# Two batches' last 64 tokens in one product with w_theta, and a new order of work around it

## The chip, the core and the metric

The program runs on one core of a Trainium2 chip. That core has five engines with an instruction stream each: TensorE (PE; matmuls and the loads of their stationary side), VectorE (DVE), ScalarE (ACT), GpSimd (POOL) and SyncE (SP), which here only issues transfers. TensorE writes its results to PSUM banks, and DVE and ACT read them from there. The metric is the device time of one execution in microseconds.

## The reference

There are 8 batches of 576 tokens. Attention comes first: 8 heads of 64 channels, keys and values averaged over groups of 8 tokens, so that 576 queries meet 72 pooled keys. The result, 576 tokens by 512 channels per batch, is the input x of a mixing block.

```python
def _attn_ref(q, k, v):                       # (8, 8, 576, 64) each
    k_p = k.reshape(B, H, 72, 8, D).mean(axis=3)
    v_p = v.reshape(B, H, 72, 8, D).mean(axis=3)
    scores = scale * np.matmul(q, k_p.transpose(0, 1, 3, 2))
    attn = softmax(scores)                    # written out with max, exp and sum
    return np.matmul(attn, v_p)

def _moe_ref(x, w_theta, w_tok_r, w_tok_i, w_ch):
    theta = x @ w_theta
    zr, zi = x * np.cos(theta), x * np.sin(theta)
    y = np.einsum('ts,bsd->btd', w_tok_r, zr) + np.einsum('ts,bsd->btd', w_tok_i, zi)
    u = x + y
    return u + np.maximum(u @ w_ch, 0.0)
```

All inputs are 32-bit floats. The product with w_theta takes a token's 512 channels to 512 angles. It is done for each token by itself, so tokens of different batches may share a product.

## The kernel before, in words

Every operand of a large product is split into a high and a low part, and three of the four partial products are added in PSUM. One "product" of a token block with w_theta (`pt`, line 888) is therefore 12 matmuls: 3 terms by 4 blocks of 128 channels. The stationary side is 128 tokens of x, the moving side 512 columns of w_theta.

The work of a batch b is written as Python generators ("streams"), each of which yields after each step. One long text, `SCHEDULE` (lines 30 to 131), names the stream whose next step comes next, and with a letter at the end (v, a or g) the engine that does it. So the order of each engine's instructions, the transfers of SP among them, is the order of the words in that text. Nothing is reordered later; an engine whose next instruction must wait holds up all that stand behind it. The words, for batch b:

- `k`, `v`, `Q` load keys, values and queries, `K` and `V` pool them and put them in place.
- `Sb.m` (`soften`): scores of token block m in bank pair `s`, maximum, exponential, sum, division, and a transpose into the buffer `G`. Blocks 0 to 3 have 128 tokens, block 4 has 64.
- `Eb.0`, `Eb.2` (`turn`): for blocks 0 and 1, or 2, 3 and 4, sixteen transfers on SP from `G` to the single buffer `eraw`, and the split into high and low.
- `Xb.g.c` (`attend`): four matmuls for channel block c, giving x (bank `av`; 256 tokens for g = 0, 320 for g = 2), then a copy out of the bank. After the last c of g = 2 the last 64 tokens are copied once more, so that block 4 of x has 128 columns, each token twice.
- `Tb.m` (`rotate`): for token block m the split of x, the product `pt` (bank `th`), its rounding on ACT and DVE (tile `g`), four transposes of x (bank `px`), sine and cosine on ACT, and the products with x into `z`. In block 4 the two copies of a token give sine and cosine at once, by a bias that differs between the two halves (`c_half`).
- `Zb.c` (`take`), `Mb.c.hf` (`mix`): the split of z, 27 matmuls with the token weights for 256 (hf = 0) or 320 tokens (hf = 1), in one of two banks `mm`, and u = x + y with its split.
- `Fb.c.hf` (`final`): 12 matmuls with w_ch, the sum, a transpose into `R`; after the second half four transfers to the output.

M of a batch reads z of all of its tokens, so it comes after all five T of the batch. The steady part of the order overlaps M and F of batch b with T of batch b + 1 and S, E and X of batch b + 2 or b + 1. The banks `av`, `th`, `px`, `s` and the tiles `g`, `sn`, `G`, `eraw` exist once; x exists twice (tag `xT`, one tile of 640 columns for each batch), the splits `xh` and `xl` of a block twice.

Of the kernel before, what the change touches and what calls it, by code (L numbers as in the profile page):

```python
# [9 lines left out]
F32 = mybir.dt.float32  # L10
# [71 lines left out]
T3.3 T3.3 T3.3 F2.2.0 F2.2.0 F2.2.1 F2.2.1 F2.2.1 V5.0g T3.3 T3.3a T3.3 E4.0g E4.0g V4g T3.3 T3.3 S4.3g S4.3g  # L82
S4.4 K5a T3.4 T3.4 T3.4 T3.4 T3.4 T3.4 F2.3.0 Q5.1 Q5.1 T3.4 F2.3.1 F2.3.1 F2.2.1 E4.0g F2.3.0 K5 K5a X4.0.0
S5.0 X4.0.0v F2.3.0 F2.3.1 X4.0.1 X4.0.1a Z3.0g Z3.0v M3.0.0 M3.0.0 S4.3 Z3.1a Z3.1g S4.4 S4.4 S4.4g S4.4g S5.0
X4.0.2 X4.0.2a S4.4 v5.1 M3.0.0v M3.0.0v V5.1g M3.0.1 M3.0.1 M3.0.1g M3.0.1g X4.0.3 X4.0.3a T4.0v T4.0v Z3.2a
Z3.2g M3.1.1 M3.1.1 M3.1.1a M3.1.1v T4.0 T4.0 T4.0 T4.0 S5.1 v5.2 V5.2g S5.0 S5.0 S5.0v S5.0v S5.1 S5.1 M3.1.0
M3.1.0 M3.1.0a M3.1.0v S5.1 Z3.3a Z3.3v T4.0 T4.0a M3.2.0 k6.0 M3.2.0 M3.2.0v M3.2.0g E4.2 E4.2g S5.0 M3.3.0
M3.3.0 M3.3.0v E4.2a E4.2g E4.2v M3.2.1 M3.2.1 X4.2.2 M3.3.0g X4.2.2a M3.2.1v F3.0.0 F2.3.1 S5.1v X4.2.0 X4.2.0a
F3.0.0 S5.1v S5.1 k6.2 K6.2v K6.0g T4.1v T4.1v M3.3.1 M3.3.1 M3.3.1g M3.3.1g X4.2.1 X4.2.1a F3.0.0 Q6.0 S5.2
S5.2 X4.2.3 k6.1 T4.0 T4.0 T4.0 V5a V5g X4.2.3v T4.1 V5 M3.2.1g K6.1g T4.1 E5.0 T4.1 T4.1 T4.1 T4.1a T4.1 T4.2v  # L90
# [40 lines left out]
"""

EARLY, EXACT, V_ON_PE, K_ON_PE, Q_ON_PE, SUMS_ON_ACT = 2, 1, 1, 1, 2, 2


@with_exitstack
def tile_attn_moe(  # L140
# [832 lines left out]
    def final(b, c, hf):  # L973
# [30 lines left out]
        if hf == 0:  # L1004
            return
# [123 lines left out]
```

## Time and profile before

| | |
|---|---|
| median of the runs | 630.47 us (630.33 to 631.11, 3 runs) |
| the profiled execution | 629.07 us, its span 627.3 us |
| TensorE busy | 591.2 us, 94% of the span, 4120 matmuls |
| DVE, ACT, POOL busy | 77%, 50%, 56% |
| granted TensorE clock, mean | 0.996 |

A row of the order of time gives the start, the time from first start to last end, the engine, the line, the operation, output and inputs with shapes, and the count of instructions merged in it. In brackets stands how long the engine was idle before it and what ended the wait. A row of a group gives busy time, the mean of one in ns, and the idle time before. Matmuls overlap, so that the distance from the start of one to the start of the next is shorter than the length of either.

### The profile page before, as it was taken

What the parts mean: (1) busy time and instruction counts of PE and PEld (TensorE: products, weight loads), DVE (VectorE), ACT (ScalarE), POOL (GpSimd) and SP (SyncE); (2) the same over time, 40 slices, a digit from 0 to 9 for tenths busy, and PEclk for the clock granted to TensorE, in tenths of its full rate; (3) what the DMA queues carried; (4) which work ended last, traced back from release to release, by engine and by line L of the source; (5) the groups of instructions that cost most, each with busy time, mean ns of one, the idle gap of its engine ahead of it and who ended that gap; (6) DMA issues with size and microseconds to landing.
All of it is one profiled execution on the core that took longest, in us unless ns stands there. A gap on an engine that the chain in (4) does not pass through costs nothing.

```text
span 627.3 us, 11459 instructions
## 1 busy us (share of the span) xinstructions
PE 591.2 (94%) x4120; PEld 545.7 (87%) x4120; DVE 481.5 (77%) x878; ACT 312.6 (50%) x674; POOL 350.2 (56%) x380
## 2 busy tenths in 40 slices
PE   4889979999899999899999999999999999999995
PEld 4766769988799879899899989989998999998995
DVE  5599988988897889878967898877886689456433
ACT  4769857688742556247534553237314451345000
POOL 5346545756484656565574667667675375611430
PEclk9999999999999999999999999999999999999999
DMA  9946212475465556554726356443362340511015
GB/s 295 266 135 190 67 43 77 81 124 118 91 125 99 98 100 125 100 95 82 129 58 108 63 107 120 75 85 56 52 100 51 68 65 5 79 20 30 9 20 77
DMA packets 235129, 57.85 MB, mean 92 GB/s; under 512 B 223168, under 2 KB 223680, under 8 KB 235072
## 3 DMA queue, kind: packets, MB, share of 16 engines
q1 hardware_dynamic: 233888, 56.97, 45.2%
q8 instruction: 33, 0.54, 0.4%
q10 hardware_dynamic: 1184, 0.15, 0.2%
q14 instruction: 24, 0.20, 0.1%
HBM read 37.81 MB, written 9.44 MB: 75 GB/s over the span
## 4 chain that ended last, share of the span: by engine, by line
PE 59%; DVE 14%; SPq 10%; DMA 7%; ACT 4%; issue 3%; POOL 3%; DVEq 0%; POOLq 0%; ACTq 0%
PE py L954 24%; PE pf L983 12%; PE pt L888 11%; SPq L814 8%; PE pv L861 4%; PE s L670 3%; DMA out_dram<-R 2%; PE px L898 2%; DMA eraw<-G 1%; DMA WTh_st<-in_moe_w_theta_dram 1%; SPq L1008 1%; DVE kpst L443 1%; DVE R L1002 1%; DMA kpst<-in_k_dram 1%; DVE xT L960 1%
## 5 line engine op out<-in xcount | busy, mean ns | idle before, releaser
L954 PE MATMUL py<-WTh,zh 128*128 128x256 f32 (+1 forms) x576 | 86.5, 297 | 4.4 <-DVE xT L960 2.8
L954 PE MATMUL py<-WTl,zh 128*128 128x256 f32 (+1 forms) x576 | 87.3, 296 | 0.0
L954 PE MATMUL py<-WTh,zl 128*128 128x256 f32 (+1 forms) x576 | 86.0, 294 | 1.0 <-DVE xT L960 1.0
L954 PEld LDWEIGHTS py<-WTh,zh 128*128 128x128 f32 x576 | 80.1, 189 | 5.3 <-DVE xT L960 3.0
L954 PEld LDWEIGHTS py<-WTl,zh 128*128 128x128 f32 x576 | 80.4, 190 | 0.0
L954 PEld LDWEIGHTS py<-WTh,zl 128*128 128x128 f32 x576 | 78.0, 188 | 1.6 <-DVE xT L960 1.2
L940 POOL TENSOR_TENSOR zl<-z,zh 128x640 fp32r<-128x640 f32 (+1 forms) x40 | 59.5, 1509 | 29.4 <-ACT zh L175 28.9
L967 POOL TENSOR_TENSOR ul<-xT,uh 128x320 fp32r<-128x320 f32 (+1 forms) x41 | 34.6, 849 | 43.6 <-DVE uh L177 29.1
L960 DVE TENSOR_TENSOR xT<-py,xT 128x256 f32<-128x256 f32 (+1 forms) x64 | 28.4, 445 | 35.1 <-PE py L954 35.0
L892 ACT ACTIVATE g<-pt,c_magic 128x512 f32<-128x512 f32 x38 | 26.1, 686 | 44.6 <-PE pt L888 36.2
L983 PE MATMUL pf<-uh,chh 128*128 128x256 f32 (+1 forms) x256 | 47.1, 305 | 0.3 <-DVE xT L960 0.3
L888 PE MATMUL pt<-th,xh 128*128 128x512 f32 x160 | 45.3, 405 | 1.4 <-DVE g L894 0.8
L983 PE MATMUL pf<-ul,chh 128*128 128x256 f32 (+1 forms) x256 | 44.8, 296 | 0.0
L983 PE MATMUL pf<-uh,chl 128*128 128x256 f32 (+1 forms) x256 | 44.5, 296 | 0.0
L894 DVE SCALAR_TENSOR_TENSOR g<-g,pt 128x512 f32<-128x512 f32 x38 | 25.8, 680 | 24.1 <-ACT g L892 23.8
L175 ACT CAST uh<-xT 128x320 fp32r<-128x320 f32 (+1 forms) x28 | 12.0, 434 | 63.2 <-DVE xT L960 63.1
L888 PE MATMUL pt<-th,xl 128*128 128x512 f32 x160 | 43.3, 393 | 0.0
L725 ACT ACTIVATE e_eps<-e_eps 128x576 f32<-128x576 f32 (+1 forms) x30 | 20.6, 686 | 45.4 <-DVE e_eps L721 45.3
L888 PE MATMUL pt<-tl,xh 128*128 128x512 f32 x160 | 43.1, 391 | 0.0
L865 ACT ACTIVATE xT<-pv 128x320 f32<-128x320 f32 (+1 forms) x41 | 16.8, 410 | 51.3 <-PE pv L861 45.6
L881 POOL TENSOR_TENSOR xl<-xT,xh 128x512 fp32r<-128x512 f32 x22 | 30.0, 1368 | 20.2 <-ACT xh L175 16.6
L989 DVE SCALAR_TENSOR_TENSOR oT<-pf,xT 128x256 f32<-128x256 f32 (+1 forms) x64 | 28.5, 449 | 14.2 <-PE pf L983 13.5
(252 smaller groups left out, 1491.6 us busy)
## 6 DMA issues: line engine op xcount, KB each, us to landing
out_dram<-R SPq DMA_DIRECT2D x112, 72.0 KB, 2.1
kpst<-in_k_dram SPq DMA_DIRECT2D x15, 512.0 KB, 3.9
vpst<-in_v_dram SPq DMA_DIRECT2D x28, 256.0 KB, 3.9
qsst<-in_q_dram SPq DMA_DIRECT2D x96, 72.0 KB, 2.4
eraw<-G SPq DMA_DIRECT2D x96, 60.0 KB, 2.2
eraw<-G SPq DMA_DIRECT2D x96, 40.0 KB, 2.1
WTh_st<-in_moe_w_theta_dram SPq DMA_DIRECT2D x4, 512.0 KB, 8.6
wcraw<-in_moe_w_ch_dram SPq DMA_DIRECT2D x4, 512.0 KB, 3.3
```

Source lines behind the costliest of these rows:

```text
L814: nc.sync.dma_start(blocks(Ex, jj, i), blocks(Gx, i, jj))
L861: nc.tensor.matmul(pv[:, :gn], l, r, start=i == 0, stop=i == len(terms) - 1)
L881: ENG[pick()].tensor_tensor(xl, xT[:, :, o], f32(xh), ALU.subtract)
L888: nc.tensor.matmul(pt, l[:, c, :], r[:, c, :], start=i == 0, stop=i == 11)
L892: nc.scalar.activation(g, pt, AF.Identity, bias=c_magic)
L894: nc.vector.scalar_tensor_tensor(g, g, MAGIC, pt, ALU.subtract, ALU.subtract)
L940: ENG[pick()].tensor_tensor(zl[:, r], z[:, r, o], f32(zh[:, r]), ALU.subtract)
L954: nc.tensor.matmul(py[:, :n], l[:, kk, :], r[:, kk, t], start=i == 0, stop=i == 3 * NK - 1)
L960: nc.vector.tensor_tensor(u, py[:, :n], u, ALU.add)
L967: ENG[pick()].tensor_tensor(ul[:, c, t], u, f32(uh[:, c, t]), ALU.subtract)
L983: nc.tensor.matmul(pv[:, :n], l[:, kk, o], uhl[r][:, kk, t], start=i == 0, stop=i == 11)
L989: nc.vector.scalar_tensor_tensor(oT, pv[:, :n], 0.0, xT[:, c, t], ALU.max, ALU.add)
```

## The change

The text `SCHEDULE` is replaced from the third step of `T3.3` on (word 1,026 of 1,884); only its very end is the same. Beside that:

- For the batches whose number halved is in `PAIRED` (b = 4 and 5, counted from 0; the fifth and the sixth) block 4 is rotated together: `rotate_pair` puts the 64 tokens of each into one block of 128, makes one product, and keeps batch 5's half of the rounded angles in the tile `kg` until `T5.4`. `turn_last` then does the transposes, a sine and a cosine for one batch, on 64 partitions each.
- x is two tiles for each batch, one of 256 columns (tokens 0 to 255) and one of 384 (the last 320 tokens and the second copy of 64). The spare tile that batch 0 uses is divided likewise.
- For batch 3 (`PART_1_FIRST`) the later 320 tokens come first in `mix` and `final`; for batch 5 the words of blocks 2, 3 and 4 (`S5.2` to `S5.4`, `E5.2`, `X5.2`) now stand ahead of those of blocks 0 and 1.
- The last parts of the keys and of the queries are loaded into `kg`, no longer into the buffer that the values share.

The words of T4.4 rise from 9 to 13, those of T5.4 fall from 9 to 5. In M, 11 of the splits move from POOL to ACT. The new order from the words before E5.2 to the first M of batch 4:

```diff
+V5g E5.2 T4.0 T4.0 T4.0 F3.1.1 F3.1.1 F3.1.1
+F3.1.0 S5.0 F3.1.0 S5.0 S5.0g S5.0v V5 V5g F3.2.1 F3.2.1 T4.0 F3.2.0 F3.3.1 T4.0 T4.0a T4.0 T4.0 T4.0 F3.1.0
+F3.1.0 F3.2.0 S5.1 E5.2a E5.2v E5.2v E5.2v F3.2.1 T4.1g F3.3.1 T4.1 V5g X5.2.0 X5.2.0v Q6.0 X5.2.3 X5.2.3a T4.1
+T4.1 T4.1 X5.2.2 X5.2.2a S5.0 X5.2.1 X5.2.1a T4.4v T4.4v X5.2.3a T4.4v T4.4v T4.1 T4.1v T4.1 F3.2.0 k6.1 K6.1g
+T4.2v T4.2g K6 K6a T4.1 T4.1 T4.4 T4.4 T4.4 T4.4g T4.4 T4.4 T4.3a Q6.1 Q6.1 T4.2 T4.4 T4.3g T4.4 T4.2 T4.4 T4.2
+T4.2 T4.2 S5.1 v6.2 v6.0 V6.2g V6.0g T4.2a T4.2 T4.2 T4.2 T4.3 T4.3 T4.3 K6 F3.2.0 K6v S6.0 T4.3 T4.3 T4.3v T4.3
+F3.3.0 T4.3 T4.3 F3.3.0 F3.3.0 F3.3.1 Z4.0a Z4.0v M4.0.0
```

and the code, cut to its core:

```diff
+PART_1_FIRST = (3,)
+PAIRED = (2,)
...
+    XPARTS = (("xTa", 256), ("xTb", XW - 256))
...
+    kg = const([P, POOL * D], F32, "kg")
...
-            st = work([64, POOL * D], F32, "kvr", f"{name}rst{b}")
+            st = kg[0:64]
...
+    def rotate_pair(b):
+
+        xh = work([P, NC, P], F32R, "xh", f"xh{b}_4", bufs=2)
+        xl = work([P, NC, P], F32R, "xl", f"xl{b}_4", bufs=2)
+        for i in range(2):
+            copy(pick(), xh[:, :, 64 * i : 64 * i + 64], xTs[b + i, 256][:, :, 256:320])
+            yield
+        for i in range(2):
+            r = slice(64 * i, 64 * i + 64)
+            ENG[pick()].tensor_tensor(xl[:, :, r], xTs[b + i, 256][:, :, 256:320], f32(xh[:, :, r]), ALU.subtract)
+            yield
+        pt = bank([P, DM], "th", f"pt{b}_4")
+        i = 0
+        for l, r in ((xh, th), (xh, tl), (xl, th)):
+            for c in range(NC):
+                nc.tensor.matmul(pt, l[:, c, :], r[:, c, :], start=i == 0, stop=i == 11)
+                i += 1
+        yield
+        g = work([P, DM], F32, "g", f"g{b}_4")
+        nc.scalar.activation(g, pt, AF.Identity, bias=c_magic)
+        yield
+        nc.vector.scalar_tensor_tensor(g, g, MAGIC, pt, ALU.subtract, ALU.subtract)
+        yield
+        copy(pick(), kg[64:128], g[64:128])
+        yield
+        yield from turn_last(b, g[0:64], c_cos[0:64])
+
+    def turn_last(b, g, quarter):
+        px = bank([P, DM], "px", f"px{b}_4")
+        for c in range(NC):
+            nc.tensor.transpose(px[:, P * c : P * c + P], xTs[b, 256][:, c, 256:384], ident)
+        yield
+        s = work([P, DM], F32, "sn", f"sn{b}_4")
+        nc.scalar.activation(s[64:128], g, AF.Sin, scale=-TWO_PI)
+        yield
+        gi = g.bitcast(I32)
+        nc.vector.tensor_scalar(gi, gi, 0x7FFFFFFF, None, ALU.bitwise_and)
+        yield
+        nc.scalar.activation(s[0:64], g, AF.Sin, scale=-TWO_PI, bias=quarter)
+        yield
...
+        nc.vector.tensor_tensor(zs[b][:, 4, :], px, s, ALU.mult)
+        yield
 
     def rotate(b, m):
...
+        if m == 4 and b // 2 in PAIRED:
+            yield from turn_last(b, kg[64:128], c_cos[64:128]) if b % 2 else rotate_pair(b)
+            return
...
-        for l, r in terms if hf == 0 else terms[::-1]:
+        for l, r in terms if hf == (b in PART_1_FIRST) else terms[::-1]:
```

More of the change, by code (lines that the diff above doesn't have):

```diff
@@ L86 @@
[L86 to L90, printed above, removed]
@@ L261, in tile_attn_moe @@
     zs = {}
-    spare = work([P, NC, XW], F32, "xT", "spare", bufs=2).rearrange("p c n -> p (c n)")
-    spare_at = {"e": (0, 576), "en": (576, 1152), "g": (1152, 1664), "sn": (1664, 2176)}
+    spares = [
+        work([P, NC, n], F32, t, f"spare{t}", bufs=2).rearrange("p c n -> p (c n)") for t, n in XPARTS
+    ]
+    spare_at = {"e": (1, 0, 576), "en": (1, 576, 1152), "g": (0, 0, 512), "sn": (0, 512, 1024)}
     signs = [stage(x, I32)[:, 2 * S : 3 * S] for x in ("chh", "chl")]
@@ L567, in queries_on_pe @@
         elif b:
-            st = work([64, DM], F32, "kvr", f"qst{b}")
+            st = kg[0:64]
         else:
@@ L841, in attend @@
         g0, tiles, gn = group(m)
-        if b not in xTs:
-            xTs[b] = work([P, NC, XW], F32, "xT", f"xT{b}", bufs=2)
+        if (b, g0) not in xTs:
+            t, n = XPARTS[g0 // 256]
+            xTs[b, g0] = work([P, NC, n], F32, t, f"{t}{b}", bufs=2)
         eh, ev, er = parts[b, g0]
-        xT, Vr = xTs[b], Vrs[b]
+        xT, Vr = xTs[b, g0], Vrs[b]
         if b == 0 and g0:
@@ new lines, in turn_last @@
+    def turn_last(b, g, quarter):
[11 more added lines that the diff above has]
+        yield
+        if b not in zs:
+            zs[b] = work([P, NK, DM], F32, "z", f"z{b}")
+        nc.vector.tensor_tensor(zs[b][:, 4, :], px, s, ALU.mult)
+        yield
@@ L989, in final @@
         nc.vector.scalar_tensor_tensor(
-            oT, pv[:, :n], 0.0, xT[:, c, t], ALU.max, ALU.add
+            oT, pv[:, :n], 0.0, xTs[b, t0][:, c, 0:n], ALU.max, ALU.add
         )
```

109 lines of the change are left out of this document (55 added, 54 removed).

## The prediction

> **What bounds the kernel now.** I read the page first, then the busy time by stretches, then TensorE's waits, then the order of its products with the time of each.
>
> ```profile
> span 627.3 us, 11459 instructions
> ...
> L888 PE MATMUL pt<-th,xh 128*128 128x512 f32 x160 | 45.3, 405 | 1.4 <-DVE g L894 0.8
> ```
>
> Busy time by stretches (length; busy time of PE, weight loads, DVE, ACT, POOL; granted clock):
>
> ```profile
> 10.00:15.00 5.00, 1.66 (x20) 1.15 (x18) 3.35 (x7) 2.98 (x7) 1.46 (x2) 0.97 1.15 318
> 15.00:20.00 5.00, 4.85 (x21) 3.40 (x22) 1.14 (x2) 3.09 (x9) 2.52 (x2) 0.69 1.12 210
> ...
> 352.43:380.12 27.69, 27.52 (x183) 24.44 (x181) 24.60 (x44) 16.23 (x28) 20.12 (x25) 1.00 0.49 93
> 380.12:620.00 239.88, 237.24 (x1679) 226.91 (x1679) 164.82 (x300) 83.17 (x141) 125.98 (x128) 1.00 0.33 55
> ```
>
> TensorE's waits from 330 us to the end:
>
> ```profile
> PE py L954 <- DVE xT L960: 1.0, 1, 1.0
> PE pv L861 <- DVE eraw L835: 1.0, 1, 1.0
> PE px L898 <- DVE z L917: 0.5, 2, 0.3
> PE pv L861 <- POOL er L828: 0.3, 1, 0.3
> ```
>
> From 330 us on, where the order changes, TensorE waits 2.8 us in all: 27.52 of 27.69 and 237.24 of 239.88 us are busy. A product taken away there is worth its whole time, and a wait put in costs its whole time. The other engines have room; what matters of them is how long a chain through them is against TensorE's work beside it.
>
> The price of a product is the distance between starts, not the record's length (405 ns in the group above, because products overlap):
>
> ```profile
> 333.39 1.24 PE L954 MATMUL py<-WTh,zh 128*128 128x256 f32 x9
> ...
> 336.57 1.24 PE L954 MATMUL py<-WTh,zh 128*128 128x256 f32 x9
> ...
> 350.27 0.31 PE L861 MATMUL pv<-eh,Vh 128*128 128x320 f32 x1
> ...
> 350.86 1.14 PE L670 MATMUL s<-kpT,qT 128*128 128x144 f32 x8
> 351.74 0.40 PE L861 MATMUL pv<-eh,Vh 128*128 128x320 f32 x1
> ...
> 352.43 1.09 PE L888 MATMUL pt<-th,xh 128*128 128x512 f32 x4
> ...
> 355.19 0.60 PE L898 MATMUL px<-ident,xT 128*128 128x128 f32 x4
> 355.54 0.83 PE L983 MATMUL pf<-uh,chh 128*128 128x320 f32 x4
> ...
> 357.38 0.64 PE L983 MATMUL pf<-uh,chh 128*128 128x256 f32 x4
> ...
> 358.82 1.07 PE L888 MATMUL pt<-th,xh 128*128 128x512 f32 x4
> ```
>
> So M (256 columns) takes 336.57 - 333.39 = 3.18 us, X 0.59, S 0.88, the theta product pt 355.19 - 352.43 = 2.76, px 0.35, F 1.84 (320) and 1.44 (256).
>
> **What is removed.** Batches are numbered from 0 here as in the code, so the pair is 4 and 5. T5.4's own product goes: 12 matmuls, 2.76 us. The pair's product still streams 512 columns twelve times; only its stationary side is full now. With it go one g and one subtraction on ACT and DVE, no gain where neither bounds.
>
> By the Trainium skill (TensorE: Matmul & The Clock Gate, Back-to-back issue gap) a sustained stream has about 131 ns for each 512-column product; the trace has 2.76 / 12 = 230 ns, so the measurement decides. By the page the saving would be 1.6 us, and the sum below would end 1.2 us higher.
>
> **What costs nothing.** x in two tiles, the load tile kg and batch 3's reversed halves change addresses and release points, no instruction. The split sine is one ACT record more in each batch of the pair (0.63 us, a row below), the copy into kg one on POOL; T5.4 reads kg many products later. Cover for both: in the 239.9 us above ACT is busy 83 and POOL 126. If that cover were gone, 2 us.
>
> **What the new order adds.** I followed TensorE's new order of words and looked at what each product must wait for. The order now wants X5.2 before T4.4, so before M4, and leaves this one sequence: X4.2.0, X4.2.1, T4.0, five F3, S5.1, T4.1, X5.2.0, X5.2.3, px, X5.2.2, X5.2.1, pk, T4.4, px, T4.2, px, T4.3, pk, S6.0, px, F3.3.0, M4.0.0. Its banks av (X), th (pt) and px are single, and so are g and eraw.
>
> (1) X straight behind X, four times (X4.2.0/1, X5.2.0/3, X5.2.2/1, X5.0.0/2): the next must wait until ACT or DVE has read av. Before never had this from batch 2 on. The nearest rows have a px of 0.35 between two X:
>
> ```profile
> 142.28 0.31 PE L861 MATMUL pv<-eh,Vh 128*128 128x320 f32 x1
> ...
> 143.07 0.44 ACT L865 ACTIVATE xT<-pv 128x320 f32<-128x320 f32 x1
> ...
> 143.56 0.41 PE L861 MATMUL pv<-eh,Vh 128*128 128x320 f32 x1
> ```
>
> Start to start 1.28, against 0.59 of work: 0.69 lost with nothing between, 0.34 with the px. Four times 0.69 is 2.76, and X5.2.3/px/X5.2.2 gives 0.34: 3.1 us. Bounds 2.8 and 3.4.
>
> (2) X5.2.0 behind E5.2's sixteen copies. They can't begin until the last X4.2 has read eraw; SP issues them in order, behind F3.0.0's stores. (Q5.1's loads, moved ahead of E4.2's copies on SP, delay nothing: E4.2 waits for S4.4's transposes anyway.)
>
> ```profile
> 352.27 0.31 PE L861 MATMUL pv<-er,Vr 96*128 96x320 f32 x1
> ```
>
> ```profile
> 352.51 10.49 SPq L814 DMA_DIRECT2D eraw<-G  x16
> ...
> 393.77 11.32 SPq L814 DMA_DIRECT2D eraw<-G  x16
> ```
>
> ```profile
> 404.76 1.90 ACT L175 CAST er<-eraw 32x320 fp32r<-32x320 f32 x4 [1.79 <-DMA eraw<-G]
> ...
> 407.02 1.52 DVE L177 CAST eh<-eraw 128x1280 fp32r<-128x1280 f32 x1 [1.23 <-DMA eraw<-G]
> ```
>
> ```profile
> L835 DVE TENSOR_TENSOR eraw<-eraw,eh 128x1280 fp32r<-128x1280 f32 x4 | 7.1, 1764 | 0.7 <-ACT eh L175 0.7
> ```
>
> The first copy starts 0.24 after the last X; the cast eh can start 407.02 - 393.77 = 13.25 after it, takes up to 1.52, and the subtraction 1.76: 16.8 us from the last X4.2 to X5.2.0's third product. TensorE has in that time 2 x 2.76 + 3 x 1.84 + 2 x 1.44 + 0.88 + 0.35 = 15.1, and 0.3 of X5.2.0. So 1.4 by these rows, and nothing if copies and casts are a tenth faster: I take 0.9, bounds 0 and 2.5. Behind E5.2's steps DVE has F3.3.1's sum and T4.1's subtraction, which frees the bank of T4.4's product some 4 us on; SP has the loads k6.1 and Q6.1, wanted only by K6 and S6.0.
>
> (3) T4.4 begins two X and one pk later, but needs batch 5's x: 0.16 until the last product has landed, 0.44 for ACT's copy, and DVE's cast, with 0.05 at each of three handovers.
>
> ```profile
> L177 DVE CAST uh<-xT 128x256 fp32r<-128x256 f32 x13 | 6.3, 484 | 0.4
> ```
>
> That is 1.23, less the pk (four small transposes, taken as one px, 0.35): 0.9. Bounds 0.5 and 1.2.
>
> (4) and (5) T4.2 behind T4.4, T4.3 behind T4.2: pt's bank is free only when ACT's g and DVE's subtraction have read it. From batch 1 on, before has 1.8 us or more of other products there (px and an F); once that was too little:
>
> ```profile
> 227.66 1.21 PE L888 MATMUL pt<-th,xh 128*128 128x512 f32 x4 [0.78 <-DVE g L894]
> ```
>
> The chain itself, T3.3's:
>
> ```profile
> 300.02 1.07 PE L888 MATMUL pt<-th,xh 128*128 128x512 f32 x4
> ```
>
> ```profile
> 302.97 0.69 ACT L892 ACTIVATE g<-pt,c_magic 128x512 f32<-128x512 f32 x1 [0.46 <-PE pt L888]
> 304.75 0.63 ACT L905 ACTIVATE sn<-g 128x512 f32<-128x512 f32 x1 [1.09 <-DVE g L894]
> ...
> 306.08 0.73 ACT L913 ACTIVATE g<-g,c_cos 128x512 f32<-128x512 f32 x1
> ```
>
> ```profile
> 304.07 0.65 DVE L894 SCALAR_TENSOR_TENSOR g<-g,pt 128x512 f32<-128x512 f32 x1
> ...
> 306.95 0.68 DVE L917 TENSOR_TENSOR z<-px,g 128x512 f32<-128x512 f32 x1
> ```
>
> g starts 2.95 after the product; with 0.69, a handover and 0.65 the bank is free after 4.35. TensorE has 2.76 and a px of 0.35: 1.25 lost. T4.4's g also stands behind K6's copies on ACT and T4.1's last z, so (4) 1.4, bounds 1.1 and 2.2; (5) 1.3, bounds 1.1 and 1.8.
>
> (6) M4.0.0 needs T4.3's z and its rounded copy zh.
>
> ```profile
> 314.47 1.15 ACT L175 CAST zh<-z 128x1152 fp32r<-128x1152 f32 x1
> ```
>
> From pt's start to the end of z it took 306.95 + 0.68 - 300.02 = 7.6, of which 0.4 was DVE's delay before 304.07; 7.2, zh 1.15 and two handovers make 8.45. Beside it TensorE has pt, a pk of 0.2, S6.0, px and F3.3.0: 2.76 + 0.2 + 0.88 + 0.35 + 1.44 = 5.6. Lost 2.8, bounds 2.0 and 4.0. Before had four F, T4.4 and X5.0.0 there, and no wait.
>
> **The sum.** 3.1 + 0.9 + 0.9 + 1.4 + 1.3 + 2.8 = 10.4 us of new waits (7.5 to 15.1). Less 2.76, and less 1.15 for waits that sit in the replaced order (the py wait of 1.0 and one of the px waits); the other 1.6, in batches 6 and 7, I leave as they are. Net +6.5. The profiled execution took 629.07 us (its span 627.3 and 1.8 around it), so 635.6 for a profile; the median shown, 630.47, is 1.4 above it, so **637.0**. By the bounds: 7.5 - 2.76 - 2.8 = +1.9 to 15.1 - 2.76 = +12.3, 632.4 to 642.8 for this case alone. Behind M4 the orders are alike: E5.0's copies have seven products, over 20 us, in front of X5.0.0.
>
> **The rivals.**
>
> - *Not slower: the stretch behind M4 gives it back.* From M4.0.0 on, 16 M of 3.18, 16 of 320 columns (3.97 in proportion), 32 F (1.44 and 1.76 in proportion, the 1.84 has a switch of shape in it), 15 pt, 15 px, 10 S and 23 X add up to about 233 us where the row has 239.9: 6.9 lost at changes of shape and small waits. The new order moves eleven casts and subtractions of M from POOL to ACT, with uh and ul earlier. If it closed all 6.9 and the waits came out at 7.5: 7.5 - 2.76 - 0.2 - 6.9 = -2.4, 628.1. It decides from about 6 of the 6.9 on. Against it: the waits shown there are only 2.6, the rest goes with shapes that stay.
> - *No change*: the same with 4.5 of the 6.9 closed, 630.5.
> - *The clock.* After the two long waits at the start TensorE is busy 1.66 of 5 us and the next 5 us have a granted clock of 0.69: 1.6 us lost. From T4.4 to M4.0.0 it would wait 0.9 + 1.4 + 1.3 + 2.8 = 6.4 of some 18 us. If the gate fell once there: 638.6. The Trainium skill (TensorE: Matmul & The Clock Gate, What's actually happening) has the clock at half after an idle window of about 3.4 us; my longest wait is below that, so the chance is small.
> - *E5.2 late.* SP's order or DVE's transposes into G start the copies 3 us later, each microsecond of it on TensorE: 640.
>
> **How the numbers follow.** Own case 0.68, not slower 0.12, no change 0.05, clock 0.07, E5.2 late 0.08. About 0.2% (1.3 us) is what a measurement can tell from no change. So faster 0.12, same 0.05, slower 0.83. The range goes down to the first rival and cuts the own case's top: 628.0 to 641.0; beside it 632.4 to 642.8 for the likeliest.
>
> **What would show it.** In the profile after: one group of twelve pt fewer on TensorE (4108 instructions); waits of pv on ACT or DVE's xT near 0.5 each; pt waiting twice on DVE's subtraction of g; a wait of py on zh above 2 us at M4.0.0; M4.0.0 starting some 12 us later than 380.12, of which 2.8 is work moved ahead of it (four X5.2 and S6.0, less X5.0.0). Wrong it would be if TensorE's waits after 330 us stayed below 6 us in all.

## The result, and the profile after

After took 637.62 us (median; 633.79 to 639.56) and before beside it 630.59 us: ratio 1.0123, 95% interval 1.0078 to 1.0168. Predicted were 637.0. Measured once more beside before, in the experiments, it is 634.32 to 629.72 us: 1.0084, 1.0050 to 1.0118. The change makes the kernel slower, by 4.6 to 7.0 us. The profiled execution took 638.62 us.

```profile
span 636.8 us, 11417 instructions
...
PE 596.1 (94%) x4108; PEld 548.1 (86%) x4108; DVE 475.2 (75%) x886; ACT 316.7 (50%) x676; POOL 337.2 (53%) x371
```

The twelve matmuls are gone (4120 to 4108), and yet TensorE is busy 596.1 us where before has 591.2. That is not more work. Most of it is the clock: in a second profile of after, without the drops shown here, it is 592.3. Busy time in stretches of the first profile of after (columns as in the prediction):

```profile
265.00:268.40 3.40, 1.48 (x11) 1.48 (x12) 3.30 (x7) 0.00 (x0) 1.74 (x2) 0.94 0.62 94
268.40:271.80 3.40, 3.40 (x19) 3.40 (x19) 2.40 (x5) 0.68 (x1) 0.82 (x1) 0.56 0.85 137
```

For 3.4 us the granted clock is half, and the same happens from 90.5 and from 373.8 us on. Each such drop costs 1.7 us at most. Two of the three lie far ahead of the changed order; the third lies in it, among the X5.2. So this execution is no good measure of the order, and I read the steps in the profile of the second measurement (632.62 us, mean clock 0.995, before's profile 0.996). Both profiles cut at T3.4's product and at M4.0.0, before first:

```profile
304.97:380.12 75.15, 74.98 (x524) 70.19 (x522) 60.88 (x113) 35.58 (x61) 47.14 (x52) 1.00 0.50 94
380.12:627.30 247.18, 237.79 (x1682) 227.25 (x1681) 165.88 (x302) 83.17 (x141) 125.98 (x128) 1.00 0.34 56
```

After, second measurement:

```profile
303.17:391.27 88.10, 80.79 (x544) 73.18 (x543) 66.41 (x126) 37.69 (x68) 47.12 (x54) 1.00 0.50 89
391.27:630.80 239.53, 232.00 (x1649) 222.25 (x1649) 154.33 (x298) 84.74 (x137) 112.91 (x117) 0.99 0.33 55
```

Up to M4.0.0 it takes 12.95 us more. 2.8 of that is work moved ahead of M4.0.0 (four X5.2 and S6.0, less X5.0.0), so 10.1 are lost. Of these, 7.1 are more idle time of TensorE (7.3 instead of 0.2) and 3.0 are more busy time for the same work: a product that starts behind a wait takes longer. T4.2's, below, takes 381.40 - 378.33 = 3.07 to the next start, T4.0's, without a wait, 354.16 - 351.39 = 2.77. Behind M4.0.0 it takes 7.65 less, 2.8 of it the moved work and 2.76 the product. From T3.4 on that is +5.3. (T3.4 itself starts 1.8 us earlier here, 2.8 later in the first profile: the early part varies from execution to execution.)

TensorE's order of time between E5.2 and M4.0.0, same profile:

```profile
349.33 0.40 PE L872 MATMUL pv<-eh,Vh 128*128 128x320 f32 x1
...
350.70 0.42 PE L872 MATMUL pv<-eh,Vh 128*128 128x320 f32 x1 [0.53 <-ACT xTb L876]
...
351.39 1.10 PE L948 MATMUL pt<-th,xh 128*128 128x512 f32 x4
...
354.16 0.74 PE L1042 MATMUL pf<-uh,chh 128*128 128x320 f32 x4
...
366.49 0.31 PE L872 MATMUL pv<-eh,Vh 128*128 128x320 f32 x1
...
367.73 0.42 PE L872 MATMUL pv<-eraw,Vh 128*128 128x320 f32 x1 [0.78 <-DVE eraw L845]
...
369.34 0.41 PE L872 MATMUL pv<-eh,Vh 128*128 128x320 f32 x1 [1.05 <-DVE xTb L878]
...
370.03 0.60 PE L958 MATMUL px<-ident,xTa 128*128 128x128 f32 x4
370.72 0.41 PE L872 MATMUL pv<-eh,Vh 128*128 128x320 f32 x1
...
372.11 0.41 PE L872 MATMUL pv<-eh,Vh 128*128 128x320 f32 x1 [0.53 <-ACT xTb L876]
...
372.79 0.60 PE L538 MATMUL pk<-ident,kp 128*64 128x128 f32 x4
373.80 1.19 PE L900 MATMUL pt<-th,xh 128*128 128x512 f32 x4 [0.42 <-DVE xh L182]
...
378.33 1.21 PE L948 MATMUL pt<-th,xh 128*128 128x512 f32 x4 [0.85 <-DVE g L906]
...
381.40 0.66 PE L958 MATMUL px<-ident,xTb 128*128 128x128 f32 x4
382.95 1.20 PE L948 MATMUL pt<-th,xh 128*128 128x512 f32 x4 [0.89 <-DVE g L954]
...
387.73 0.51 PE L680 MATMUL s<-kpT,qT 128*128 128x144 f32 x2 [0.64 <-DVE kpT L182]
...
391.27 1.33 PE L1013 MATMUL py<-WTh,zh 128*128 128x256 f32 x9 [1.16 <-ACT zh L180]
```

Here are the prediction's six steps one behind the other: X behind X (350.70, 369.34, 372.11), X5.2.0's third matmul waiting for the eraw subtraction (367.73), T4.4 for batch 5's x (373.80), T4.2 and T4.3 for the bank (378.33, 382.95), M4.0.0 for zh (391.27). One wait was not in it: S6.0's for a copy of the keys (387.73).

### The profile page after: what moved, and what is told of

Its sections match the earlier page's. It is cut to its first block, busy times and chain, and to the rows that moved or that the text cites. A ratio compares the mean times of both kernels' runs of the same rounds, so it can differ in the third digit from the quotient of the medians.

```text
span 636.8 us, 11417 instructions
## 1 busy us (share of the span) xinstructions
PE 596.1 (94%) x4108; PEld 548.1 (86%) x4108; DVE 475.2 (75%) x886; ACT 316.7 (50%) x676; POOL 337.2 (53%) x371
## 4 chain that ended last, share of the span: by engine, by line
PE 59%; DVE 16%; SPq 8%; DMA 6%; ACT 4%; issue 3%; POOL 3%; DVEq 0%; POOLq 0%; ACTq 0%
PE py L1013 24%; PE pf L1042 12%; PE pt L948 9%; SPq L824 7%; PE pv L872 5%; PE s L680 3%; DMA eraw<-G 2%; PE px L958 2%; DMA WTh_st<-in_moe_w_theta_dram 1%; DVE kpst L453 1%; DMA wraw<-in_moe_w_tok_i_dram 1%; DVE sm L737 1%; DMA out_dram<-R 1%; DVE en L742 1%; DMA kpst<-in_k_dram 1%
## 5 line engine op out<-in xcount | busy, mean ns | idle before, releaser
L1013 PE MATMUL py<-WTl,zh 128*128 128x256 f32 (+1 forms) x576 | 88.3, 299 | 0.0
L1000 POOL TENSOR_TENSOR zl<-z,zh 128x640 fp32r<-128x640 f32 (+1 forms) x36 | 53.8, 1516 | 39.1 <-ACT zh L180 38.6
L1042 PE MATMUL pf<-uh,chh 128*128 128x320 f32 (+1 forms) x256 | 46.7, 303 | 0.3 <-DVE xTa L1019 0.3
L1042 PE MATMUL pf<-ul,chh 128*128 128x320 f32 (+1 forms) x256 | 44.8, 296 | 0.0
L1042 PE MATMUL pf<-uh,chl 128*128 128x320 f32 (+1 forms) x256 | 44.4, 296 | 0.0
L735 ACT ACTIVATE e_eps<-e_eps 128x576 f32<-128x576 f32 (+1 forms) x30 | 20.6, 686 | 40.0 <-DVE e_eps L731 39.8
L680 PE MATMUL s<-kpT,qT 128*128 128x144 f32 x256 | 37.6, 289 | 2.2 <-DVE qT L182 1.6
L1042 PEld LDWEIGHTS pf<-uh,chh 128*128 128x128 f32 x256 | 37.7, 189 | 1.9 <-DVE xTa L1019 0.5
L1042 PEld LDWEIGHTS pf<-ul,chh 128*128 128x128 f32 x256 | 37.8, 190 | 0.3 <-POOL ul L1026 0.3
L714 DVE TENSOR_REDUCE mx<-s 128x8 f32<-128x576 f32 (+2 forms) x42 | 30.0, 717 | 10.4 <-PE s L680 10.3
L1042 PEld LDWEIGHTS pf<-uh,chl 128*128 128x128 f32 x256 | 37.6, 189 | 0.0
L742 POOL TENSOR_TENSOR en<-e_eps,ri 128x512 f32<-128x512 f32 (+1 forms) x18 | 19.9, 1103 | 33.5 <-DVE ri L739 21.5
```

Of the source, the lines that this page charges most:

```text
L680: nc.tensor.matmul(scs[c // 2][:n, 2 * SP * (c % 2) : 2 * SP * (c % 2 + 1)], qT[:, c, t0 : t0 + n], kpT[:, c, :], start=True, stop=True,)
L714: nc.vector.tensor_reduce(mxv, scv, AX.X, ALU.max)
L735: nc.scalar.activation(e[:n], e[:n], AF.Exp, scale=scale)
L742: ENG[pick()].tensor_tensor(en[:n, 0:512].rearrange("p (h g) -> p h g", h=8), e[:n, :, 0:GM], ri[:n].unsqueeze(2).broadcast_to([n, 8, GM]) ...
L1000: ENG[pick()].tensor_tensor(zl[:, r], z[:, r, o], f32(zh[:, r]), ALU.subtract)
L1013: nc.tensor.matmul(py[:, :n], l[:, kk, :], r[:, kk, t], start=i == 0, stop=i == 3 * NK - 1)
```

## The experiments

**The code without the order.**

```diff
-PART_1_FIRST = (3,)
-PAIRED = (2,)
+PART_1_FIRST = ()
+PAIRED = ()
 SCHEDULE = (the text of before)
```

> This kernel has the changed code (x in two tiles, the load tile kg, the functions of the pair) with the order of before, no pair and batch 3's halves as before: the code without the order. Theory (the waits of the new order set the loss): as before, 630.5 us, within 0.6, TensorE's waits from 330 us to the end near the 2.8 us of before, a mean granted clock of 0.996 as before. Rival (the code itself costs, by the two tiles or by what the copies wait for): 632 or more. Second question, on the granted clock: the profile after has three drops to 0.50 for 3.4 us each, two of them (at 90.7 and 268.4 us) behind waits of 2.25 and 2.04 us that stand in the order of before too, as 2.26 and 2.77 us. If drops follow any wait of that length by chance, some runs here are at 0.990 and 1.5 us or more longer; if they come with the new order, none.

629.46 us beside 628.91 of before, ratio 1.0009 (0.9980 to 1.0037), and TensorE's waits from 330 us on are 2.9 us, before's 2.8. The two tiles and kg cost nothing that can be told; the loss comes with the new order. (Batch 3's reversed halves, the split sine and the copy into kg are not in this kernel, so it says nothing of them.) And the clock question is answered: these executions have mean clocks from 0.988 to 0.994. In 71 executions of before in the four comparisons the mean clock goes from 0.999 to 0.986 and the time from 625.45 to 634.08 us, 0.53 us for each 0.001 (straight line through them). The drops belong to before as well.

**After once more, beside before.**

> After itself, unchanged, beside before on the same chip. In the comparison with the old order before took 625.5 to 634.1 us, at a mean granted clock of 0.997 down to 0.986: the drops come in before as well. So the earlier difference of 7.0 us holds an unequal share of drops. If it does, after is here 5 to 6 us above before, and at equal clock (0.994 in both) about 6; if the new order brings more drops, 7 or more, with after's mean clock lower than before's by 0.003 or more. The copy with the waits filled took 634.5 at 0.994; after at 0.994 should be within 1 us of it.

634.32 to 629.72 us, 4.6 us. Executions at the same clock: from 0.9945 to 0.9965 before has 627.4 (median of 8), after 633.9 (4); from 0.9885 to 0.9905, 630.9 (9) and 636.6 (3). So the order costs 5.7 to 6.5 us at equal clock. The mean clock is 0.9914 for before and 0.9908 for after over all, no difference that can be told; after has only 12 executions, in which some drops more or fewer would not stand out. In the first comparison after's mean clock was 0.988, lower than this by about one drop (3.4 us at half clock are 0.0027 of an execution), and so the 7.0 there is the larger number.

**The order without the pair.**

```diff
-T4.4v T4.4v X5.2.3a T4.4v T4.4v T4.1 ... F4.2.1 T5.4 T5.4 K7.1g T5.4 T5.4 T5.4
+T4.4v X5.2.3a T4.4v T4.1 ... T5.4g F4.2.0 F4.2.0 T5.4g F4.2.1 T5.4 T5.4 T5.4 T5.4 T5.4 K7.1g T5.4 T5.4
-PAIRED = (2,)
+PAIRED = ()
```

> The order of after, but T4.4 and T5.4 have each their own product again (T5.4's twelve matmuls stand where its transposes stood). Theory (a removed product is worth its distance between starts, 2.76 us; without the pair T4.4 need not wait 0.42 us for batch 5's x): 2.3 us more than after at the same granted clock, so 636.1 at 0.996, and 2.76 + 0.35 in the place of T5.4. Rival (the sustained figure of 131 ns for each product): 1.6 - 0.4 = 1.2 more, 635.0. Rival (T5.4's product is covered): the same as after, 633.8.

639.21 us, 1.0174 of before (1.0130 to 1.0218). At equal clock it is 2.9 to 3.9 over after. In its profile M4.0.0 starts at 392.63, so the rest takes 636.1 - 392.63 = 243.5 us, 3.9 more than after's 239.5. T5.4's product, back in its place, and one new wait, of an F behind it, are in that:

```profile
450.45 1.09 PE L945 MATMUL pt<-th,xh 128*128 128x512 f32 x4
...
453.21 0.60 PE L955 MATMUL px<-ident,xTb 128*128 128x128 f32 x4
...
457.20 0.85 PE L1039 MATMUL pf<-uh,chh 128*128 128x320 f32 x4 [1.04 <-DVE oT L1045]
```

The product takes 453.21 - 450.45 = 2.76 between starts, as said, and the new wait is 1.04; together they are about the 3.9. The 1.6 of the rival is too little. T4.4's wait for batch 5's x is gone, as expected, but M4.0.0 comes no earlier for it (88.3 us from T3.4's product to M4.0.0, in after 88.1). The saving is real. It doesn't pay for its order.

**The products spread out.** The same products, T4.4 last. The first attempt, as the order of TensorE's products (not the words of the text; some px are left out):

```diff
-X4.2.0 X4.2.1 T4.0 [five F3] S5.1 T4.1 X5.2.0 X5.2.3 px X5.2.2 X5.2.1 pk T4.4 T4.2 T4.3 S6.0 F3.3.0 M4.0.0
+X4.2.0 X4.2.1 T4.0 F3.1.1 F3.1.0 T4.1 F3.2.1 S5.1 T4.2 F3.3.1 X5.2.0 T4.3 X5.2.3 X5.2.2 pk X5.2.1 F3.2.0 T4.4 F3.3.0 S6.0 M4.0.0
```

> The pair stays; between E5.2's copies and M4.0.0 the same products stand in another order: T4.0, T4.1, T4.2 and T4.3 each with an F3, a score product or an X5.2 behind its product, X5.2.0 behind T4.2, T4.4 last. Nothing is added or taken out. Theory (steps 1 to 5 are latencies that the order leaves uncovered): T4.2's and T4.3's waits (0.86 and 0.90), X5.2.0's and X5.2.3's (0.76 and 1.06) and T4.4's (0.42) go, M4.0.0's stays (T4.4 is now the last before it, 5.6 us of products beside a chain of some 8): TensorE's waits from 330 us on fall from 8.8 to about 5, time 4 us under after at the same clock, so 629.8 at 0.996. Rival (the copies and casts of E5.2 set the end of the stretch, whatever the order): X5.2.0 or X5.2.3 waits 2 us or more and the time is within 1 us of after. Rival (the loss is the clock's): the same time as after, with drops at the same rate.

649.29 us, 1.0322 (1.0284 to 1.0359): a bad miss, by the queues of the other engines.

```profile
401.10 2.29 PE L677 MATMUL s<-kpT,qT 128*128 128x144 f32 x8 [8.50 <-DVE e_eps L728]
```

I had left S5.1's subtraction, which frees S6.0's bank, on VectorE behind Q6.1's transpose, and that waited for a load issued late on SP. With such waits in it the run says nothing on the theory. Mended (words of the text, first attempt against the mended one):

```diff
-... Q6.1 Q6.1 T4.4g S5.1 K6 K6v T4.4 ...
+... X5.2.0 X5.2.0a Q6.1 K6.1g T4.2a T4.2 T4.3 S5.1 ... T4.4 F3.2.0 F3.2.0 Q6.1 T4.4 ...
-T4.1g ... E5.2a T4.1 T4.1 Q6.0 V5g E5.2v E5.2v E5.2v
+T4.1v ... E5.2a E5.2g T4.2 T4.3a E5.2g E5.2v
```

> The spread order once more, the engines' queues mended. In the first one TensorE's products stood as meant, but S6.0 waited 8.5 us behind Q6.1's load, T4.1 1.7 us for an xl on GpSimd, T4.3 2.6 us for its xh on ScalarE, X5.2.0 2.2 us for VectorE. Now S5.1's steps stand ahead of Q6.1's transpose and Q6.1's load ahead of the stores; T4.1's xl is on VectorE, T4.3's xh ahead of T4.2's g, E5.2's small casts on GpSimd; S5.0 stands between X4.2.0 and X4.2.1. Theory (steps 1 to 5 are latencies left uncovered by the order of the products): TensorE's waits from 330 us on fall from 8.8 to 3 to 4 us, with M4.0.0's wait on T4.4's z and zh of 2 to 3 the largest; 4 to 6 us under after, so within 1.5 us of before. Rival (E5.2's copies and casts set the end of the stretch): X5.2.0 waits 2 us or more still, and the time is within 1.5 us of after.

631.01 us; before 629.72 beside it, ratio 1.0023 (0.9996 to 1.0050). By the medians 3.3 of after's 4.6 us are won back with the same products in another order (five steps beside them are also on another engine). But the mean clock was higher here, 0.9931 against 0.9914 of before beside it. At equal clock (0.9945 to 0.9965) it is 630.3 (4 executions), after 633.9 and before 627.4: 3.6 of 6.5 are won back. In the profiles, from T3.4's product to the end, it takes 324.3 us, after 327.6 and before 322.3. From T4.0's product to M4.0.0 it takes 387.79 - 352.51 = 35.3 us, after 391.27 - 351.39 = 39.9. The waits on `g` are gone, and so is X5.2.0's. What is left there:

```profile
374.53 0.63 PE L955 MATMUL px<-ident,xTb 128*128 128x128 f32 x4 [0.65 <-DVE z L974]
375.54 0.41 PE L869 MATMUL pv<-eh,Vh 128*128 128x320 f32 x1 [0.39 <-ACT xTb L873]
...
383.43 0.51 PE L677 MATMUL s<-kpT,qT 128*128 128x144 f32 x2 [0.56 <-DVE qT L562]
...
387.79 1.34 PE L1010 MATMUL py<-WTh,zh 128*128 128x256 f32 x9 [1.15 <-ACT zh L177]
```

So steps 2 to 5, and part of step 1, are latencies that after's order leaves uncovered, as the theory has it, and the rival's wait of 2 us at X5.2.0 isn't there. The sizes were not as expected: TensorE's waits from 330 us on are 5.1 us instead of 3 to 4, and M4.0.0's is 1.15 instead of 2 to 3, as S6.0 waits in the same stretch.

**One cover moved.**

```diff
-T4.4 ... Q6.1 Q6.1 T4.2 ... T4.3v T4.3 F3.3.0 T4.3 T4.3 F3.3.0
+T4.4 ... Q6.1 Q6.1 F3.3.0 T4.2 ... T4.3v T4.3 T4.3 T4.3 F3.3.0
```

> After, with one product moved: F3.3.0's (1.44 us) from in front of M4.0.0 to between T4.4 and T4.2, its sum and the rest where they were. Theory (a wait here is the latency of a chain less the products beside it): T4.2's wait of 0.85 goes and T4.2 starts 0.59 later behind T4.4 than in after (5.1 instead of 4.53); T4.3's wait of 0.9 stays; M4.0.0's wait grows from 1.16 by the whole 1.44 to 2.6; M4.0.0 is 0.6 later in all, so a cover moved forward loses a little. Rival (M4.0.0's wait has another cause than the chain through T4.3's z and zh, so it doesn't grow): it stays near 1.2 and M4.0.0 is 0.85 earlier.

One execution, read by its trace alone (T4.4, T4.2, T4.3, M4.0.0):

```profile
380.50 1.20 PE L897 MATMUL pt<-th,xh 128*128 128x512 f32 x4 [0.41 <-DVE xh L179]
...
385.45 1.07 PE L945 MATMUL pt<-th,xh 128*128 128x512 f32 x4
...
389.94 1.20 PE L945 MATMUL pt<-th,xh 128*128 128x512 f32 x4 [1.14 <-DVE g L951]
...
398.26 1.35 PE L1010 MATMUL py<-WTh,zh 128*128 128x256 f32 x9 [2.59 <-ACT zh L177]
```

T4.2's wait is gone, and M4.0.0's grew from 1.16 to 2.59, by 1.43 for a product of 1.44. From T4.4 to M4.0.0 it is 17.76 us instead of 17.47, 0.3 more where 0.6 was expected. A wait here is a chain's latency less the products beside it, and M4.0.0's chain is the one named.

**The waits filled.**

```diff
+L.mm.3 X5.2.0 X5.2.0v Q6.0 L.mm.4 X5.2.3 ... L.av.3 T4.2 ... L.av.3 T4.3 ... L.av.4 M4.0.0
+nc.tensor.matmul(p, th[:, 0, 0:P], th[:, 0, :], ...)   # n times for L.bank.n
```

> After, with products added in front of the waiting instructions, whose results nobody reads: 512 columns each, 230 ns, as many as the wait holds (X4.2.1 2, X5.2.0 3, X5.2.3 4, X5.2.1 2, T4.4 1, T4.2 3, T4.3 3, M4.0.0 4, X5.0.2 1, the X7.2 product at 552 us 4, the M2 product at 266.9 us 8). Theory (the granted clock drops where TensorE idles some 1.8 us within 3.4): no drop at 268 or 374 us, runs at 0.993 to 0.996 and 633.8 to 635, with a spread below 2 us where after has 633.8 to 639.6. Rival (drops have nothing to do with these waits): the same drops and spread as after, 637.6 as the median. Rival (the waits are not free to fill): 2 us or more over after at the same clock.

634.49 us, 1.0086 (1.0051 to 1.0122), as after's 1.0084. T4.0 to M4.0.0 takes 39.8 us as without the fill: the waits were free to fill, and so the other engines set this stretch. The clocks are 0.993 to 0.996 (after 0.984 to 0.995), the spread 3.5 us, not below 2. The steadier clock, 0.994 in the mean against 0.992, should be worth 1 us by the line above; it doesn't show in the median, and why is open. (After was measured in another comparison, each beside before.)

**X pairs taken apart.**

```diff
-S5.0 S5.0 X4.2.0 X4.2.0a X4.2.1 ... M4.2.1 M4.2.1 Z4.3a Z4.3v X5.0.0 X5.0.0a Q7.0 X5.0.2
+X4.2.0 X4.2.0a S5.0 S5.0 X4.2.1 ... X5.0.0 X5.0.0a M4.2.1 M4.2.1 Z4.3a Z4.3v Q7.0 X5.0.2
```

> After, with two of the four X pairs taken apart and nothing else: S5.0's score product goes between X4.2.0 and X4.2.1, and X5.0.0 goes ahead of M4.2.1. Theory (step 1): each pair costs its wait of 0.5 plus what the restart costs, so X4.2.1 and X5.0.2 have no wait and the time is 1.2 us under after. Rival (what is won at X4.2.1 is lost at X5.2.0's wait on the eraw subtraction, since E5.2 follows the last X4.2): X5.2.0's wait grows from 0.76 by some 0.8 and the time is 0.4 to 0.6 under after.

638.36 us, 1.0135 (1.0102 to 1.0168), slower than after; both expectations fail. X4.2.0 now stood straight behind X4.2.3 and waited 0.53 there, and

```profile
414.53 0.58 PE L869 MATMUL pv<-eraw,Vh 128*128 128x256 f32 x1 [3.19 <-POOL eraw L842]
```

X5.0.0, moved ahead by one product of 3.97, waits 3.19 for E5.0's subtraction. The cover that I thought ample there had 0.8 us to spare. And this wait has the clock behind it:

```profile
414.30:417.70 3.40, 3.17 (x12) 3.17 (x13) 2.28 (x4) 1.42 (x2) 1.45 (x2) 0.52 0.55 152
```

**T5.2 ahead of M4.0.0.** On the mended spread order:

```diff
+... T5.2g T5.2g F3.3.0 F3.3.0 F3.3.1 T5.2 Z4.0a Z4.0v T5.2 T5.2 M4.0.0 ... X5.0.3a T5.2 T5.2 T5.2a T5.2 T5.2 T5.2 S6.2
+X5.0.0 X5.0.0a M4.2.1 M4.2.1 Z4.3a Z4.3v Q7.0 X5.0.2
```

> The mended spread order, with three moves more: X5.0.0 ahead of M4.2.1, and T5.2's product (whose tokens lie in part 1 of batch 5, whose x is there already) ahead of M4.0.0, with its z written once batch 4's z is read. Theory (step 6: M4.0.0 waits for the last z and zh, and 2.76 us of other products in front of it cover that): M4.0.0's wait of 2 to 3 falls below 0.5, another 2.5 us under the mended spread order, and since T5.4's product is gone the kernel ends 1 to 2.8 us under before. Rival (the work taken ahead was the cover of a later wait, in T5.1 to T5.3 or at X6.0): the gain at M4.0.0 comes back as waits of PE between 400 and 470 us, and the time is within 1 us of the mended spread order.

651.32 us, 1.0331 (1.0296 to 1.0366). T5.2's xh stood on GpSimd behind the pooling of v, which waits for its load, and kept TensorE 7.03 us. Then two kernels beside each other: the spread order mended further, and on it T5.2 ahead with its queues mended.

```diff
-X4.2.2a F3.0.1 F3.0.1 F3.0.1 k6.2 X4.2.3 X4.2.3a ... Q6.0 X5.2.0 ... S5.1 T4.2 T4.2 ... K6 K6v S6.0
+X4.2.2a X4.2.3 F3.0.1 X4.2.3a F3.0.1 F3.0.1 k6.2 ... X5.2.0 X5.2.0a Q6.0 ... T4.2 T4.2 S5.1 ... K6 K6v T4.4 ... S6.0
```

> The mended spread order, mended further by what its trace shows. It waits 0.53 at X4.2.0 straight behind X4.2.3 (now F3.0.1 stands between), 0.65 at T4.3's px for T4.2's last z (now ahead of Q6.0's transpose and S5.1's steps on VectorE), 0.56 and 0.31 at S6.0 for Q6.1's transpose and the last key copy (both now earlier), and 1.15 at M4.0.0. Theory (each wait taken away is worth itself, until the chain from T4.4 to M4.0.0, about 8.2 us, is the only limit): the first two go, worth 1.4; at S6.0 the 0.87 goes but comes back at M4.0.0, whose wait grows to 1.5 to 2.5; 1.5 to 2 us under the mended spread order, so 0.3 to 0.8 us under before at equal clock, which is no difference that can be told. Rival (the waits in the stretch no longer set the end): no change against the mended spread order.

635.40 us, 1.0087 (1.0060 to 1.0115); slower than the order it was to mend, and the expectation failed. S6.0's waits are gone, but M4.0.0 waits 2.88 us instead of 1.15: from T4.4's product to M4.0.0 it is 8.75 us as it was 8.68, the chain alone. X5.2.0 waits for eraw again (0.98), and X4.2.3 for X4.2.2's copy (1.04). Two things make the loss. The order itself is slower: from T3.4's product to M4.0.0 it takes 85.4 us instead of 83.5. And the mean clock fell from 0.993 to 0.989. (At 0.995 one execution has 631.1 and four of the order before it have 630.3, too few to part the two.) Behind the single long wait:

```profile
388.60:392.00 3.40, 0.53 (x5) 0.29 (x4) 2.10 (x5) 2.17 (x3) 0.05 (x1) 1.00 0.67 119
392.00:395.40 3.40, 3.40 (x18) 3.40 (x18) 2.12 (x4) 2.72 (x3) 1.74 (x4) 0.52 1.17 224
```

On this order, T5.2 ahead:

```diff
+T5.2a T5.2g T4.4 ... T5.2 Z4.0a Z4.0v M4.0.0 S5.1 S5.1 S5.1g S5.1g Z4.1a T5.2 T5.2 ... T5.0a T5.0v T5.2 T5.2 T5.2a T5.2 T5.2 T5.2
+E6.0 T5.1g T5.1 ... T5.3 T5.3 T5.3 T5.3 E6.0v E6.0g
```

> The same order with T5.2's product ahead of M4.0.0, again, with what failed the first time mended: its xh stood on GpSimd behind the loads of v (7.0 us), its z ahead of X5.0.1's copy on VectorE (2.9), E6.0's cast ahead of F4.0.1's sum on VectorE (2.7), and X5.0.0 was 3.2 us earlier than E5.0's subtraction (2.8 and 1.4). Now xh is on ScalarE ahead of the pair's product, z behind X5.0.1's copy, E6.0's copies ahead of T5.1 with the cast behind T5.3's subtraction, and X5.0.0 stands where it stood. Theory (step 6 is a cover too short): M4.0.0's wait falls below 0.5, 1.5 to 2.5 us under the kernel beside it, and so 2 to 3 us under before, about the worth of T5.4's product. Rival (the cover was needed later): new waits of 1.5 us or more between 400 and 480 us, and no gain.

636.61 us, 1.0104 (1.0065 to 1.0143). M4.0.0 doesn't wait at all, as expected, but nothing is gained, as the rival has it: the waits come back behind it. They are not quite the rival's, which named 1.5 us or more between 400 and 480 us; the largest, 1.6, is at 397, and the three behind it are 2.85 together:

```profile
388.16 1.33 PE L1010 MATMUL py<-WTh,zh 128*128 128x256 f32 x9
...
397.16 1.30 PE L1010 MATMUL py<-WTh,zh 128*128 128x256 f32 x9 [1.60 <-DVE xTa L1016]
...
430.40 1.22 PE L677 MATMUL s<-kpT,qT 128*128 128x144 f32 x8 [0.84 <-DVE e_eps L728]
...
432.92 1.20 PE L945 MATMUL pt<-th,xh 128*128 128x512 f32 x4 [0.87 <-DVE g L951]
...
448.28 0.85 PE L1039 MATMUL pf<-uh,chh 128*128 128x320 f32 x4 [1.14 <-DVE oT L1045]
```

**Before, with its three longest waits filled.**

```diff
+L.th.9 W3 Q1.4a ... L.th.5 M1.0.0 ... L.av.11 M2.3.0
```

> Before itself, with products whose results nobody reads in front of its three longest waits: 9 of 512 columns (2.07 us) ahead of the wt product that waits 2.26 us at 90.8, 11 (2.5 us) ahead of the M2 product that waits 2.77 us at 265.7, 5 (1.15 us) ahead of the M1 product that waits 1.40 us at 169.4. In the runs so far before took 625.5 to 634.1 us with a mean granted clock from 0.998 down to 0.986, some 0.5 to 0.6 us for each 0.001. Theory (an idle wait of some 2 us of TensorE is what sets off a drop of 3.4 us to half clock, in those executions in which it falls into one window): the mean clock rises from 0.991 to 0.995 or more, the spread shrinks below 4 us, and the median falls by 1.5 to 2.5 us, to about 627: it would beat both kernels. Rival (drops come by chance or by heat and not by these waits): mean clock 0.991, the same spread, a median as before's or up to 0.5 us above it for the products added.

627.79 us beside 629.97: ratio 0.9961 (0.9933 to 0.9990), faster than both kernels. The mean clock is 0.9954 (0.992 to 0.998) and before's 0.9918 (0.986 to 0.999). The M2 product starts where it did (265.79, before 265.66):

```profile
263.15 2.80 PE L1091 MATMUL fill_av<-th 128*128 128x512 f32 x11
265.79 1.24 PE L951 MATMUL py<-WTh,zh 128*128 128x256 f32 x9
```

The gain goes with the clock: by the line above, 0.0036 more are worth 1.9 of the 2.2 us. So waits of this length do set off drops. The spread stayed at 6.9 us, which I had expected below 4.

## Why the prediction was right, point by point

Lost on each step, from start to start in the second profile of after, less the products between:

| step | predicted | measured |
|---|---|---|
| (1) X behind X | 3.1 | 4.0: 0.8 (X4.2.1), 1.3 (X5.2.3), 0.4 (X5.2.2, a px between), 0.8 (X5.2.1), 0.7 (X5.0.2) |
| (2) X5.2.0 and E5.2 | 0.9 | 0.9 |
| (3) T4.4 and batch 5's x | 0.9 | 373.80 - 372.79 - 0.35 = 0.7 |
| (4) T4.2 | 1.4 | 378.33 - 373.80 - 3.11 = 1.4 |
| (5) T4.3 | 1.3 | 382.95 - 378.33 - 3.11 = 1.5 |
| (6) M4.0.0 | 2.8 | 391.27 - 382.95 - 5.6 = 2.7, of it 0.64 as S6.0's wait |
| sum | 10.4 | 11.2 |

- *The waits.* All six are where the prediction put them and end on what it named. One sign failed: M4.0.0's own wait is 1.16, not above 2, though the loss of the step is the predicted one; 0.64 of it is waited at S6.0, the rest is products that take longer. By the rows (2) came to 1.4; the 0.9 was chosen between that and nothing, and that it fits is luck. The worst single wait is X5.2.3's 1.05, twice what a pair has. The prediction said that F3.3.1's sum stands on DVE behind E5.2's steps, and didn't charge it: here it goes ahead of the copy out of av.
- *S6.0's wait for the keys* was missed as a place; it lies inside (6)'s chain and adds nothing.
- *The removed product*: 2.76 predicted, 2.76 between starts in the order without the pair. The sustained 131 ns of the Trainium skill (TensorE: Matmul & The Clock Gate, Back-to-back issue gap) would give 1.6 as an estimate, and the trace does not agree for this product.
- *What costs nothing*: for the two tiles and the load tile so it is, 1.0009. The reversed halves, the split sine and the copy into kg were not run by themselves; the mended spread order has all of them and is 1.3 us over before, 2.9 at equal clock, waits included.
- *Behind M4.0.0* the order was said to be alike but for 1.15 of removed waits and X5.0.2. It gains 2.05 beside the product: 1.3 in waits (2.6 of before from 380 us to the end, 1.3 here), 0.6 in the time behind TensorE's last product, the rest in small pieces. This is the mis-sized term, 1.6 us. It goes the way of the first rival, at about a third of the 6 us that rival needed; whether by its cause, the splits moved to ACT, was not tested.
- *The sum.* Predicted +6.5 on the profiled execution; +5.3 in the trace from T3.4 on, 5.7 to 6.5 at equal clock, 4.6 and 7.0 as medians. That the first median is within 0.6 of 637.0 is luck: its executions had a mean clock of 0.988, and at the clock of the second comparison the kernel is at 634.3.
- *The sentence on E5.0* ("over 20 us") held for the order as it is, with 0.8 to spare.
- *The clock rival* was priced right (1.6 for one drop, 1.7 at most by the rows) and argued wrong. A drop did come in the first profile, at 373.8 us behind X5.2's waits, so ahead of T4.4; between T4.4 and M4.0.0 neither profile has one. By the Trainium skill (TensorE: Matmul & The Clock Gate, What's actually happening) it takes an idle window of about 3.4 us; here a wait of 2.04 us did it, and the length of the drop, 3.4 us, agrees. No difference between the kernels can be told from it, since before has waits of 2.26 and 2.77 us and drops of its own.
- *E5.2 late*: not seen.

## What to carry over

Price a moved product by the chain that must pass beside it: the distance between two users of a single bank or tile is at least the latency of its readers, and whatever products the order puts beside it are free; what is missing is lost on the bounding engine, and a little more, since the product behind a wait takes longer (3.07 instead of 2.77 us here). A cover moved only moves the wait, so look for the shortest chain cover in the new order first, and for the queues of the other engines next. And when executions of one kernel spread by more than a per cent, compare them at equal granted clock before reading a difference of a per cent.

## What the runs showed of the hardware that I hadn't expected

A wait of TensorE of about 2 us or more can be followed by 3.4 us at a granted clock of 0.5: after 2.04 and 2.25 us in after, 2.59 with one cover moved, 2.88 in the spread order mended further, 3.19 with the X taken apart. It doesn't always follow: before's profile has the clock whole behind 2.77 us. The traces show what decides. In every one of the 14 profiles the drops start at whole multiples of 3.413 us from one another (in after at 90.48, 267.98 and 373.79 us, 52 and 31 times 3.413 apart), and they last 3.413 us or a multiple of it, but for the last of a profile, which its end cuts off. So there are windows of this length that run on by themselves. Cut at these windows, after's wait of 2.04 us lies in one, in which TensorE is busy 1.38 us:

```profile
264.56:267.98 3.42, 1.38 (x12) 1.17 (x11) 3.35 (x6) 0.00 (x0) 1.97 (x3) 1.00 0.60 90
267.98:271.39 3.41, 3.41 (x19) 3.41 (x18) 2.79 (x6) 0.68 (x1) 0.62 (x2) 0.50 0.81 132
```

Before's wait of 2.77 us is shared by two windows, busy 2.43 and 1.62 us:

```profile
260.45:263.87 3.42, 2.43 (x18) 2.21 (x17) 3.42 (x1) 0.00 (x0) 3.41 (x3) 1.00 0.58 90
263.87:267.28 3.41, 1.62 (x13) 1.62 (x14) 3.27 (x8) 0.00 (x0) 0.88 (x1) 1.00 0.61 91
267.28:270.69 3.41, 3.41 (x30) 3.41 (x29) 3.36 (x7) 1.48 (x3) 0.97 (x1) 1.00 0.83 135
```

Counted over the 14 profiles, all windows of this kind from 100 to 600 us that are at full clock themselves: all 14 windows in which TensorE is busy 1.4 us or less have a drop behind them, of the two at 1.6 and 1.7 us one has, and of the 2,014 at 1.75 us or more none has. So a wait counts if enough of it falls into one window, and shorter waits add up: the third drop of after stands behind X5.2's waits of 0.76 and 1.06 us, in the window busy 1.70. In the first 100 us drops also come behind windows busy up to 2.7 us; why is open. Tested by a change is only that products without a purpose in three waits made the kernel 0.4% faster. Why the spread of times stays as wide as it was is open.
